# Attention and a feed-forward layer in one kernel: q and k loaded straight into the layout that the transposes read, and a planner with new deadlines

## The chip, the cores and the metric

The kernel runs on one core of a Trainium2 chip. The metric is the time of one execution on the device, in microseconds (us), the median of three runs. The profile comes from one further execution, which took 375.98 us; its span, from the first to the last instruction, is 374.2 us.

The engines of the core work side by side and meet at semaphores. TensorE (PE in the profile; PEld is its loading of weights) does matrix products into the PSUM buffers. VectorE (DVE) and ScalarE (ACT) take results out of PSUM and do elementwise work. GpSimd (POOL) issues most of the loads here, SyncE (SP) the transposing DMAs and the stores.

## The reference

The first half is an attention without softmax, for 8 batches, 12 heads, 448 positions and head size 64. The second is a feed-forward layer (768 to 2048 to 768) with an exact gelu over its 3,584 rows.

```python
scores = scale * np.matmul(q, k.transpose(0, 1, 3, 2))       # scale = 1 / sqrt(64)
attn = np.maximum(scores, 0.0) ** 2 / S                      # S = 448
attn_out = np.matmul(attn, v)
x = attn_out.transpose(0, 2, 1, 3).reshape(B * S, H * D)     # 3584 x 768
h = x @ w_in
g = 0.5 * h * (1.0 + erf(h / sqrt(2)))
out = g @ w_out
```

Inputs and output are float32; the kernel computes in bf16 with float32 sums.

## The kernel before

**Attention.** Heads are taken four at a time, so a batch has three groups (g = 0, 1, 2), and the keys of a group in seven blocks (i = 0 to 6). One step is one (batch, group, block): four score matmuls (`ps<-qT,kT`, L623) into a PSUM buffer named "w" in the planner, a relu with the scale that brings them to SBUF (`a_sq<-ps`: L635 on ScalarE, L637 on VectorE), and a square on VectorE (`a_sq<-a_sq`, L644). After seven steps come 28 matmuls with v (`pav`, L683), also into a "w" buffer, and two copies to `xT`. There are three "w" buffers.

**Feed-forward.** The first product (`psh`, L730) with its gelu (L740) fills a ring `h_sb` of two batches. The second (`pso`, L1036) works on groups of 256 output rows, by a scheme of seven products in place of eight (p1 to p7, in the order p1, p6, p2, p7, p5, p4, p3), with sums of h halves and of weight quarters formed on VectorE. Results pass through output buffers `osb` (L1070) and go out by DMA. The PSUM buffers of these are named "f"; there are two. The last two batches use the same seven-product scheme for their first product as well (`add_blocks`, `add_block`: matmuls `pb`, L870; passes `part`, L904; gelu L913). There a batch gives 28 atoms of six matmuls, 14 for each half of the hidden units; in a half each of the products p1, p6, p2, p7, p5, p4, p3 stands twice, for the two column halves of one "w" buffer. A pass takes a partial result out of a bank before the next product adds to it: v1 copies p1, v2 and v3 follow p6 and p7, and p4 goes into the bank that v3 has read.

**q, k and v.** Scores need q and k with the head dimension on partitions. Batches 0 and 1 are transposed on TensorE. Batches 2 to 7 take another way: GpSimd issues three DMAs that load and cast q, k and v of a batch (tiles `nq`, `nk`, `v_sb`). VectorE permutes q and k in SBUF (`pq<-nq`, L477, six copies in a batch; `pk<-nk`, L466, three copies) so that two heads lie side by side in 128 columns. SyncE then issues seven transposing DMAs (`kT<-pk`, L569, three; `qT<-pq`, L578, four). `pq` and `pk` have one buffer each, `qT` and `kT` two. After the transposes of a batch a small copy on GpSimd, the gate (L590), waits for their end; behind it stand the loads of the next batch but one after the batch that is being computed.

**The order.** A planner in Python (`Scheduler`) decides, while the program is built, in which order each engine gets its instructions. It has a model of durations. The first part, to about 50 us, is written out by hand (`ORDER`). From batch 2 on TensorE's order is fixed too: the score steps of a batch stand in six slots, two to a group (four steps with the v product of the group before in the middle, then three), and feed-forward work is spread evenly between them. In the last two batches `woven` mixes the `pb` atoms with `pso` products. What is left to the planner is the order on VectorE and ScalarE, and which of the two takes a relu or copy: each operation lists its engines, and a relu on VectorE, its second choice, is charged `RELU_DVE`, 0.8 us. From the second pass on, the choice among operations that can start within `NEAR` goes to the earliest deadline (`self.late`), which `deadlines` works out backwards from TensorE's sequence. The DMAs on GpSimd keep their written order; at most eight of them are under way at once. What the engines wait for on the chip is set by the data alone, not by the planner's times.

Of the kernel before, what the change touches and what calls it, by code (L numbers as in the profile page):

```python
# [51 lines left out]
TSUM_BIAS = 0.2  # L52
LEADS = {3: 8}
LAST = 256
PASSES = 2
NEAR = 0.5
QUEUE_STEP = 1.5
LOAD_MARGIN = 2.0


def cols(half):
# [41 lines left out]
class Scheduler:  # L103
# [39 lines left out]
    def pick(self, ops, only=None):  # L143
        top, near = None, []
        for n, op in enumerate(ops):
            t = self.ready(op)
            if t is None:
                continue
            for x, (eng, dur, lat) in enumerate(op.engines):
                if self.late and only not in (None, eng):  # L150
                    continue
                est = max(t, self.free[eng])
                if isinstance(lat, tuple):
                    est = max(est, self.landed[-8])
                if eng == "PE" and op.mode != self.mode:
                    est += SWITCH
                key = (est + op.bias + x * op.other, n)
                if top is None or key < top[0]:
                    top = (key, est, op, eng, dur, lat)
                near.append((est + x * op.other, est, n, op, eng, dur, lat))  # L160
        if top and self.late and only in ("ACT", "DVE"):
            edge = min(near)[0] + NEAR
            top = min(
                ((self.late[id(o)], n), est, o, eng, dur, lat)
                for at, est, n, o, eng, dur, lat in near if at <= edge
            )
        return top
# [26 lines left out]
    def run(self, fixed):  # L194


        for _ in range(PASSES):
            self.reset()
            self.place(fixed)
            self.deadlines()  # L200
        self.open = []
        n = len(ORDER.split())
        for est, op, eng in self.log[:n] + sorted(self.log[n:], key=lambda x: x[0]):
            op.fn(eng)

    def deadlines(self):


        after = {id(o): [] for o in self.open}
        for o in self.open:  # L210
            for d in o.deps:
                if id(d) in after:
                    after[id(d)].append(o)
                elif isinstance(getattr(d, "op", None), Op):
                    after[id(d.op)].append(o)
        takers = {}
        for _, o, _ in self.log:
            for name in o.need:
                takers.setdefault(name, []).append(o)
        for name, v in self.given.items():  # L220
            n = self.buffers[name]
            for x, o in enumerate(v):
                if x + n < len(takers[name]):
                    for y in [o] + list(o.joint):
                        after[id(y)].append(takers[name][x + n])
        self.late = {}
        t = math.inf
        order = sorted(self.log, key=lambda x: x[0])
        pe = [o for _, o, e in order if e == "PE"]
        ideal, at = {}, 0.0  # L230
        for o in pe:
            ideal[id(o)] = at
            at += o.engines[0][1]
        shift = pe[-1].start - ideal[id(pe[-1])]
        queue = math.inf
        for est, o, e in reversed(order):
            t = ideal[id(o)] + shift if e == "PE" else est + 50.0
            if e == "SP" and o.mode == "X":
                t = min(t, queue - QUEUE_STEP)
            for s in after[id(o)]:  # L240
                if id(s) in self.late:
                    t = min(t, self.late[id(s)] - (o.done - o.start))
            if e == "SP" and o.mode == "X":
                queue = t
            self.late[id(o)] = t
# [38 lines left out]
def kernel(  # L284
# [55 lines left out]
    def kv_view(t, b, g0, g1):  # L340

        return t[b, 4 * g0 : 4 * g1].rearrange("h s d -> (h s d)").rearrange(
            "(x p f) -> p x f", p=128, f=NK * D
        )
# [21 lines left out]
    def get_p():  # L366
        if not pqk:
            pqk.append(natpool.tile([KC, NC, DM], BF16, tag="pq", name="pq"))
            pqk.append(natpool.tile([128, G, NK * 128], BF16, tag="pk", name="pk"))
        return pqk  # L370
# [29 lines left out]
    def dma(fn, nbytes, deps=(), issues=1):  # L400
        op = sch.add((("POOL", 0.7 * issues, (nbytes, issues)),), lambda e: fn(), deps)
        pool_q.append(op)
        return op
# [7 lines left out]
    def war(b):  # L411

        old = [o for (bb, *_), o in list(Pq.items()) + list(Pk.items()) if bb == b - 1]
        c = {1: -1, 2: 0}.get(b, b - 1)
        old += [o[0] for (bb, *_), o in list(Tq.items()) + list(Tk.items()) if bb == c]
        return old

    def add_k(b, g0, g1):
        def fn():
            get_nat(b)  # L420
            nc.gpsimd.dma_start(nk[b][:, 2 * g0 : 2 * g1], kv_view(k, b, g0, g1))

        o = dma(fn, (g1 - g0) * 4 * S * 256, war(b))
        for g in range(g0, g1):
            ld_k[b, g] = [o] * NK
# [10 lines left out]
    def add_v(b, g0, g1):  # L436
# [6 lines left out]
        for g in range(g0, g1):  # L443
            ld_v[b, g] = [o]

    def add_load(b, g0=0, g1=G):
        add_k(b, g0, g1)
        add_q(b, g0, g1)
        add_v(b, g0, g1)
# [29 lines left out]
    def add_pk(b, g0, g1, after=(), bias=0.0):  # L479
        for g in range(g0, g1):  # L480
            deps = ld_k[b, g] + list(after)
            deps += [Tk[max(b - 1, 1), x, i][0] for x in range(G) for i in range(NK)]
            Pk[b, g] = sch.add(
                (("DVE", 0.31, 0.43),),
                lambda e, g=g: permute_k(V.tensor_copy, g, nk[b][:, 2 * g : 2 * g + 2]), deps,
                bias=bias,
            )

    def add_pq(b, g0, g1, c0=0, c1=NC, after=(), bias=0.0):
        for g in range(g0, g1):  # L490
            deps = [ld_q[b, g, c] for c in range(c0, c1)] + list(after)
            deps += [Tq[max(b - 1, 1), g, c][0] for c in range(c0, c1)]
            if b == 2:
                deps += [Tq[1, x, c][0] for x in range(G) for c in range(NC)]
            d = 2 * (0.07 + (c1 - c0) * 128 / 3840)

            def fn(e, g=g):
                permute_q(
                    V.tensor_copy, g, c0, c1, nq[b][:, 4 * g : 4 * g + 4, c0 * D : c1 * D]
                )  # L500

            op = sch.add((("DVE", d, d + 0.12),), fn, deps, bias=bias)
            for c in range(c0, c1):
                Pq[b, g, c] = op
# [354 lines left out]
    def add_block(b, m4, y, ms, bank, x, t, TS, xs, old, half):  # L859
# [39 lines left out]
        def passed(name, to, other, deps, need=()):  # L899
            def fn(e):  # L900
                if other is None:
                    copy(e, get(to), ps(name))
                else:
                    V.tensor_add(get(to), ps(name), get(other))  # L904

            eng = e_copy(S, 1)
            return sch.add(eng if other is None else eng[:1], fn, deps, need=need, bias=PASS_BIAS)

        def gelu(src, r, c, deps, frees=()):
            def fn(e):  # L910
# [376 lines left out]
    def at(b, n):  # L1287
        return [at_slot(b, n)]
# [5 lines left out]
    for b in range(2, B):  # L1294
        add_steps(steps(b), dve=True)
        if b == 2:
            x1 = f1(1)
            first_atoms = x1[:LEAD]
            flow += x1[LEAD:]
            flow += [(2.6, add_plain(t, n)) for n in (1, 0) for t in (0, 1)]  # L1300
            add_tsums()
        elif b in F1B:
            flow += f1(F1B[b])
        if b + 1 < B:

            n = {2: 2, 3: 2}.get(b, 1)
            add_pk(b + 1, 0, G, after=at(b, n) + SUMS[0] + SUMS[1])
            add_pq(b + 1, 0, G, after=at(b, n) + SUMS[0] + SUMS[1])
            add_T_dma(b + 1, [at(b, n + (y >= 4)) for y in range(7)])
            if b + 2 < B:  # L1310
                add_gate(b + 1)
                add_load(b + 2)
        flow += [y for g in GROUPS.get(b, ()) for y in add_group(g)]
    add_wsums(at(B - 1, 1), [F1[B - 3, m, None] for m in range(KF)])

    def woven(x, y, n):


        tx, ty, gone, out = sum(o[0] for o in x), sum(o[0] for o in y[:n]), 0.0, []
        k = 0  # L1320
        for o in x:
            out.append(o)
            gone += o[0]
            while k < n and (k + 0.5) / n < gone / tx:
                out.append(y[k])
                k += 1
        return out + y[k:]

    end = woven(add_blocks(B - 2), add_group(9), 4)
    g10 = add_group(10)  # L1330
    end += g10 + woven(add_blocks(B - 1), add_group(11), 4)
    end += add_group(12) + add_group(13)
    pe_q.extend(x[1] for x in first_atoms)
    share, gone, edge = sum(x[0] for x in flow) / (B - 2), 0.0, 0.0
# [50 lines left out]
```

## Time and profile before

| | |
|---|---|
| time, median of 3 (lowest to highest) | 376.32 us (376.17 to 376.45) |
| span of the profiled execution | 374.2 us |
| TensorE's granted clock, mean | 1.000 |
| DMA packets | 69,685, of which 30,512 on the queue of GpSimd |
| idle before the gate copies, for the transposes | 155.6 us in 5 waits |

```profile
DVE  3998981799848787985889768946888879785762
ACT  4998864746337865666546575657562333035100
PEclk9999999999999999999999999999999999999999
DMA  9999999997579969989333799400020201210233
q0 software_dynamic: 30512, 22.47, 40.2%
q1 hardware_dynamic: 38768, 19.46, 25.5%
L635 ACT ACTIVATE a_sq<-ps 128x896 bf16<-128x896 f32 (+1 forms) x143 | 122.8, 914 | 57.5 <-PE ps L623 57.5
L637 DVE TENSOR_SCALAR a_sq<-ps 128x896 bf16<-128x896 f32 x26 | 28.2, 1088 | 28.5 <-PE ps L623 28.1
L590 POOL COPY gate<-qT 128x4 bf16<-128x4 bf16 x5 | 1.3, 266 | 155.6 <-DMA qT<-pq 155.6
nk<-in_k_dram POOLq DMA_DIRECT2D x5, 672.0 KB, 6.7
nq<-in_q_dram POOLq DMA_DIRECT2D x5, 672.0 KB, 9.3
v_sb<-in_v_dram POOLq DMA_DIRECT2D x5, 672.0 KB, 13.4
```

In the first four lines the span is cut into 40 slices of some 9.4 us, and a digit is the busy share in tenths (for PEclk the granted clock). The queue lines give packets, MB and the time of the packets as a share of 16 DMA engines' span. In a line of a group of instructions there stand after the bar the busy time and the mean duration in ns, and after the second bar the idle time just before them with what ended it. In the last three, the size of one DMA and the median time from its issue to its landing.

### The profile page before, as it was taken

How to read it: one execution, taken by the hardware profiler on the slowest of the kernel's cores; microseconds unless marked ns; L12 is line 12 of the kernel's file. 1: busy time of each engine (PE TensorE's matmuls, PEld its weight loads, DVE VectorE, ACT ScalarE, POOL GpSimd, SP SyncE). 2: the span in 40 equal slices, each digit the busy share in tenths (PEclk: the TensorE clock that was granted, in tenths of full speed). 3: DMA queues.
4: the chain of work that ended last, by engine and by line, in shares of the span. 5: the costliest groups of instructions: out<-in, count | busy, mean ns of one | idle time of the engine just before them, and what ended most of it. 6: DMA issues, size and time to landing. Idle time of an engine off the chain costs nothing.

```text
span 374.2 us, 8324 instructions
## 1 busy us (share of the span) xinstructions
PE 363.0 (97%) x3485; PEld 215.4 (58%) x3485; DVE 284.3 (76%) x517; ACT 200.9 (54%) x301; POOL 46.0 (12%) x69
## 2 busy tenths in 40 slices
PE   8799999999999999999999999999999999999995
PEld 7566645455554455544555445544555886688663
DVE  3998981799848787985889768946888879785762
ACT  4998864746337865666546575657562333035100
POOL 8666400300002011002000020000000000000000
PEclk9999999999999999999999999999999999999999
DMA  9999999997579969989333799400020201210233
GB/s 175 195 201 204 202 190 114 171 205 143 94 171 162 146 75 190 238 113 159 64 101 79 140 154 181 120 3 0 2 86 12 75 2 31 90 49 2 85 86 84
DMA packets 69685, 42.96 MB, mean 115 GB/s; under 512 B 37776, under 2 KB 66192, under 8 KB 69648
## 3 DMA queue, kind: packets, MB, share of 16 engines
q0 software_dynamic: 30512, 22.47, 40.2%
q1 hardware_dynamic: 38768, 19.46, 25.5%
q8 instruction: 27, 0.44, 0.5%
q10 hardware_dynamic: 368, 0.51, 0.4%
q14 instruction: 10, 0.08, 0.1%
HBM read 45.61 MB, written 11.01 MB: 151 GB/s over the span
## 4 chain that ended last, share of the span: by engine, by line
PE 84%; DVE 6%; ACT 4%; issue 2%; DMA 2%; POOL 1%; DVEq 0%; ACTq 0%; POOLq 0%
PE pso L1036 32%; PE psh L730 29%; PE ps L623 8%; PE pb L870 7%; PE pav L683 4%; ACT a_sq L635 4%; PE pso L1131 3%; DVE a_sq L644 3%; DVE part L904 2%; DMA nk<-in_k_dram 2%; DVE a_sq L637 1%; DVE xT L387 0%; DVE kT L387 0%; PE tp L517 0%; ACT xT L389 0%
## 5 line engine op out<-in xcount | busy, mean ns | idle before, releaser
L635 ACT ACTIVATE a_sq<-ps 128x896 bf16<-128x896 f32 (+1 forms) x143 | 122.8, 914 | 57.5 <-PE ps L623 57.5
L730 PE MATMUL psh<-xT,win_sb 128*128 128x448 bf16 (+1 forms) x612 | 114.2, 342 | 0.1
L644 DVE TENSOR_TENSOR a_sq<-a_sq 128x896 bf16<-128x896 bf16 (+1 forms) x169 | 98.7, 615 | 11.2 <-ACT a_sq L635 10.1
L730 PEld LDWEIGHTS <-win_sb 128*128 128x128 bf16 x612 | 57.4, 98 | 53.7 <-issue 9.2
L740 ACT ACTIVATE h_sb<-psh 128x448 bf16<-128x448 f32 x96 | 52.5, 547 | 34.3 <-PE psh L730 34.0
L1036 PEld LDWEIGHTS <-s_sb 128*128 128x128 bf16 x424 | 40.6, 98 | 27.7 <-issue 2.5
L623 PE MATMUL ps<-qT,kT 64*64 64x448 bf16 (+1 forms) x756 | 48.5, 336 | 3.1 <-ACT a_sq L635 0.7
L637 DVE TENSOR_SCALAR a_sq<-ps 128x896 bf16<-128x896 f32 x26 | 28.2, 1088 | 28.5 <-PE ps L623 28.1
L1036 PEld LDWEIGHTS <-h_sb 128*128 128x128 bf16 x312 | 29.8, 98 | 20.9 <-issue 2.4
L1036 PE MATMUL pso<-wout_sb,h_sb 128*128 128x384 bf16 x208 | 38.1, 326 | 0.0
L1036 PE MATMUL pso<-t_sb,s_sb 128*128 128x384 bf16 x208 | 38.1, 326 | 0.0
L1036 PE MATMUL pso<-wout_sb,s_sb 128*128 128x384 bf16 (+2 forms) x216 | 38.1, 320 | 0.0
L683 PE MATMUL pav<-a_sq,v_sb 64*64 64x448 bf16 (+1 forms) x756 | 36.8, 330 | 0.8 <-ACT a_sq L635 0.4
L623 PEld LDWEIGHTS <-kT 64*64 64x64 bf16 x756 | 18.6, 105 | 26.9 <-issue 21.3
L1070 DVE TENSOR_TENSOR osb<-pso,p_sb 128x384 f32<-128x384 f32 x39 | 21.6, 555 | 9.5 <-PE pso L1036 7.3
L683 PEld LDWEIGHTS <-v_sb 64*64 64x64 bf16 x756 | 21.1, 107 | 13.1 <-issue 2.3
L387 DVE CAST xT<-pav 128x448 bf16<-128x448 f32 (+1 forms) x44 | 24.3, 582 | 5.5 <-PE pav L683 4.9
L904 DVE TENSOR_TENSOR part<-pb,part 128x448 f32<-128x448 f32 x40 | 23.1, 618 | 6.3 <-PE pb L870 6.2
L913 ACT ACTIVATE h_sb<-part 128x448 bf16<-128x448 f32 x24 | 13.3, 577 | 18.4 <-DVE part L904 18.3
L590 POOL COPY gate<-qT 128x4 bf16<-128x4 bf16 x5 | 1.3, 266 | 155.6 <-DMA qT<-pq 155.6
L870 PEld LDWEIGHTS <-win_sb 128*128 128x128 bf16 x192 | 18.4, 98 | 3.2 <-issue 2.1
L1036 PE MATMUL pso<-t_sb,h_sb 128*128 128x384 bf16 x104 | 19.0, 326 | 0.0
(60 smaller groups left out, 262.1 us busy)
## 6 DMA issues: line engine op xcount, KB each, us to landing
nk<-in_k_dram POOLq DMA_DIRECT2D x5, 672.0 KB, 6.7
nq<-in_q_dram POOLq DMA_DIRECT2D x5, 672.0 KB, 9.3
v_sb<-in_v_dram POOLq DMA_DIRECT2D x5, 672.0 KB, 13.4
out_dram<-osb SPq DMA_DIRECT2D x8, 336.0 KB, 3.1
wout_sb<-in_moe_w_out_dram POOLq DMA_DIRECT2D x2, 1152.0 KB, 11.7
v_sb<-in_v_dram POOLq DMA_DIRECT2D x9, 224.0 KB, 9.0
out_dram<-osb SPq DMA_DIRECT2D x7, 288.0 KB, 3.1
out_dram<-osb SPq DMA_DIRECT2D x8, 240.0 KB, 2.8
```

The source lines that it names most:

```text
L387: V.tensor_copy(dst, src)
L623: nc.tensor.matmul(ps[64 * j : 64 * j + 64, e, x * w : x * w + w], kT[r, g, i * 128 + 64 * j : i * 128 + 64 * j + 64], qT[r, 2 * g + j, co ...
L635: A.activation(ar, ps, AF.Relu, scale=c_att)
L637: V.tensor_scalar(ar, ps, c_att, 0.0, op0=mybir.AluOpType.mult, op1=mybir.AluOpType.max,)
L644: V.tensor_mul(box["a2"][:, :, :used], ar, ar)
L683: nc.tensor.matmul(pav[0][o2 : o2 + 64, e, :w], vt[b][r, 2 * g + e, bass.ts(i, D)], box["a2"][r, e, o : o + w], start=(i == 0), stop=(i == ...
L730: nc.tensor.matmul(ph[:, x * n : x * n + n], win_sb[:, kd, bass.ts(m + x, 128)], xT[b][:, kd, c], start=(kd == 0), stop=(kd == KD - 1),)
L740: A.activation(h_ring()[:, m : m + nm, o + c.start : o + c.stop], box[0][:, :S].rearrange("p (x n) -> p x n", x=nm), AF.Gelu,)
L870: nc.tensor.matmul(bank[name][:, y, z * HS : z * HS + HS], w[:, k, bass.ts(mm, 128)], right()[:, k], start=first and k == 0 and z == 0, st ...
L904: V.tensor_add(get(to), ps(name), get(other))
L1036: nc.tensor.matmul(box[bank][:, n0:n1], left()[:, kf], right[:, kf, n0:n1], start=bool(need) and kf == 0, stop=kf == K2 - 1, skip_group_ch ...
L1070: V.tensor_add(out()[:, n0:n1], box[bank][:, n0:n1], other()[:, n0:n1])
```

## The change

**Loads.** `add_load` of batches 3 to 7 becomes `add_wide`. It loads q and k from DRAM straight into `pq` and `pk`, 64 elements at a time: six DMAs for k (two places of a head in a pair, three groups), twelve for q, and one for v as before. The permuting copies of these batches (`add_pk`, `add_pq`) and their tiles are dropped; the transposes wait for the DMAs instead (`Both` stands for several DMAs as one). Batch 2 keeps its copies. `WIDE` is the factor by which the planner reckons such a load dearer.

**Deadlines.** `deadlines` took each TensorE operation's ideal time from the sum of the durations before it, shifted to end with the last one. It now takes the end of the operation just before it in the last pass, that is, the time at which it could start without a wait. `limit` is the latest end of each operation. A relu's charge for VectorE falls away when its first engine, ScalarE, would end more than `LIMIT` past that. There are five passes instead of two, and the one in which TensorE ends earliest is used. A transpose's deadline gets a margin of 5 us.

**The end.** `woven` puts one `pso` product behind the fourth and tenth of each 14 atoms, where it went by summed durations before. The first copies (v1) in the blocks may run on ScalarE alone, where both engines were allowed.

```diff
-PASSES = 2
+PASSES = 5
+LIMIT = 0.1
+QUEUE_MARGIN = 5.0
+WIDE = 2.0
...
-                near.append((est + x * op.other, est, n, op, eng, dur, lat))
+                other = op.other
+                if x and self.late:
+                    first = max(t, self.free[op.engines[0][0]]) + op.engines[0][2]
+                    if first > self.limit[id(op)] + LIMIT:
+                        other = 0.0
+                near.append((est + x * other, est, n, op, eng, dur, lat))
...
+            end = self.free["PE"]
+            if best is None or end < best[0]:
+                best = (end, list(self.log))
...
             ideal[id(o)] = at
-            at += o.engines[0][1]
-        shift = pe[-1].start - ideal[id(pe[-1])]
+            at = o.start + o.engines[0][1]
...
-            t = ideal[id(o)] + shift if e == "PE" else est + 50.0
+            t = ideal[id(o)] if e == "PE" else est + 50.0
...
-                    t = min(t, self.late[id(s)] - (o.done - o.start))
+                    m = QUEUE_MARGIN if e == "SP" and o.mode == "X" else 0.0
+                    t = min(t, self.late[id(s)] - (o.done - o.start) - m)
+            self.limit[id(o)] = t + (o.done - o.start)
...
+    def add_wide(b):
...
+                to = get_p()[1].rearrange("p g (i e d) -> e p g i d", e=2, d=D)
+                src = kv_view(k, b, 0, G).rearrange("p (g e) (i d) -> e p g i d", e=2, d=D)
+                for g in range(G):
+                    nc.gpsimd.dma_start(to[e][:, g], src[e][:, g])
...
+                to = get_p()[0].rearrange("p c (g j e d) -> j e g p c d", j=2, e=2, d=D)
+                src = q[b].rearrange("(g e j) (p c) d -> j e g p c d", e=2, j=2, c=NC)
+                for g in range(G):
+                    nc.gpsimd.dma_start(to[j][e][g], src[j][e][g])
...
     def add_load(b, g0=0, g1=G):
+        if b > 2:
+            return add_wide(b)
...
-            return sch.add(eng if other is None else eng[:1], fn, deps, need=need, bias=PASS_BIAS)
+            return sch.add(eng[1:] if other is None else eng[:1], fn, deps, need=need, bias=PASS_BIAS)
...
-            add_pk(b + 1, 0, G, after=at(b, n) + SUMS[0] + SUMS[1])
-            add_pq(b + 1, 0, G, after=at(b, n) + SUMS[0] + SUMS[1])
...
-            while k < n and (k + 0.5) / n < gone / tx:
-                out.append(y[k])
-                k += 1
+            if n % 14 in (3, 9):
+                out.append(y.pop(0))
```

More of the change, by code (lines that the diff above doesn't have):

```diff
@@ L194, in run @@
     def run(self, fixed):
+        best = None
         for _ in range(PASSES):
@@ L200, in run @@
             self.deadlines()
-        self.open = []
+            end = self.free["PE"]
+            if best is None or end < best[0]:
+                best = (end, list(self.log))
+        self.open, self.log = [], best[1]
         n = len(ORDER.split())
@@ L225, in deadlines @@
                         after[id(y)].append(takers[name][x + n])
-        self.late = {}
-        t = math.inf
+        self.late, self.limit = {}, {}
         order = sorted(self.log, key=lambda x: x[0])
@@ L444, in add_v, with k_fn, fn, q_fn @@
             ld_v[b, g] = [o]
+    def add_wide(b):
+        def k_fn(e):
+            def fn():
+                to = get_p()[1].rearrange("p g (i e d) -> e p g i d", e=2, d=D)
+                src = kv_view(k, b, 0, G).rearrange("p (g e) (i d) -> e p g i d", e=2, d=D)
+                for g in range(G):
+                    nc.gpsimd.dma_start(to[e][:, g], src[e][:, g])
+            return fn
+        def q_fn(e, j):
+            def fn():
+                to = get_p()[0].rearrange("p c (g j e d) -> j e g p c d", j=2, e=2, d=D)
+                src = q[b].rearrange("(g e j) (p c) d -> j e g p c d", e=2, j=2, c=NC)
+                for g in range(G):
+                    nc.gpsimd.dma_start(to[j][e][g], src[j][e][g])
+            return fn
+        def v_fn():
+            vt[b] = vpool.tile([128, HP, NK * D], BF16, tag="v", name="v_sb")
+            nc.gpsimd.dma_start(vt[b], kv_view(v, b, 0, G))
+        n = G * 4 * S * 256
+        ks = [dma(k_fn(e), WIDE * n / 2, war(b), G) for e in range(2)]
+        qs = [dma(q_fn(e, j), WIDE * n / 4, war(b), G) for e in range(2) for j in range(2)]
+        old = [o for (bb, *_), o in AV.items() if bb == b - 3]
+        o = dma(v_fn, n, old)
+        ops = Both(ks), Both(qs)
+        for g in range(G):
+            ld_v[b, g] = [o]
+            Pk[b, g] = ops[0]
+            for c in range(NC):
+                Pq[b, g, c] = ops[1]
+    class Both:
+        def __init__(self, ops):
+            self.ops = ops
+        @property
+        def done(self):
+            ends = [o.done for o in self.ops]
+            return None if None in ends else max(ends)
     def add_load(b, g0=0, g1=G):
+        if b > 2:
+            return add_wide(b)
         add_k(b, g0, g1)
@@ L1314, with woven @@
     add_wsums(at(B - 1, 1), [F1[B - 3, m, None] for m in range(KF)])
[L1316 to L1321, printed above, removed]
+    def woven(x, y):
+        out, y = [], list(y)
+        for n, o in enumerate(x):
             out.append(o)
-            gone += o[0]
-            while k < n and (k + 0.5) / n < gone / tx:
-                out.append(y[k])
-                k += 1
-        return out + y[k:]
-    end = woven(add_blocks(B - 2), add_group(9), 4)
+            if n % 14 in (3, 9):
+                out.append(y.pop(0))
+        return out + y
+    end = woven(add_blocks(B - 2), add_group(9))
     g10 = add_group(10)
-    end += g10 + woven(add_blocks(B - 1), add_group(11), 4)
+    end += g10 + woven(add_blocks(B - 1), add_group(11))
     end += add_group(12) + add_group(13)
```

## The prediction

> **What bounds the kernel now.** I read the engine totals and the row of 40 slices first, then the chain of work that ended last, then windows and the timeline around each place where that chain leaves TensorE. In the totals TensorE is busy for 97% of the span, VectorE for 76%; ScalarE's 54% falls to a third or less near the end.
>
> ```profile
> PE 363.0 (97%) x3485; PEld 215.4 (58%) x3485; DVE 284.3 (76%) x517; ACT 200.9 (54%) x301; POOL 46.0 (12%) x69
> ...
> PE 84%; DVE 6%; ACT 4%; issue 2%; DMA 2%; POOL 1%; DVEq 0%; ACTq 0%; POOLq 0%
> ```
>
> So only what shortens TensorE's gaps counts. Gaps before 31 us lie in the hand-written opening order, which the change leaves alone. From there to about 290 us the chain is an unbroken row of matmuls, but for ten detours of this shape:
>
> ```profile
> 140.79 0.60 issue
> 141.39 0.92 ACT a_sq L635
> 142.36 0.38 PE ps L623 x4
> ```
>
> The timeline around this one shows their size:
>
> ```profile
> 140.14 0.57 PE L623 MATMUL ps<-qT,kT 64*64 64x448 bf16 x8
> 140.29 0.55 DVE L1070 TENSOR_TENSOR osb<-pso,p_sb 128x384 f32<-128x384 f32 x1
> ...
> 140.58 2.62 ACT L635 ACTIVATE a_sq<-ps 128x896 bf16<-128x896 f32 x3 [0.86 <-PE ps L623]
> 140.76 0.68 DVE L1017 TENSOR_TENSOR s_sb<-s_sb,h_sb 128x1024 bf16<-128x1024 bf16 x1
> ...
> 141.87 0.87 PE L623 MATMUL ps<-qT,kT 64*64 64x448 bf16 x8
> ```
>
> The same eight score matmuls take 0.57 us at 140.14 and 0.87 us at 141.87: the second group of four waits for a "w" buffer whose relu is the second in ScalarE's queue. That is 0.30 us, ten times: **3.0 us**. (They stand near 89, 124, 132, 142, 154, 191, 204, 241, 265 and 278 us.)
>
> In the blocks of the last two batches the gaps end at VectorE:
>
> ```profile
> 331.62 1.31 PE L870 MATMUL pb<-xs,ws 128*128 128x224 bf16 x12
> 331.82 2.84 DVE L904 TENSOR_TENSOR part<-pb,part 128x448 f32<-128x448 f32 x5 [0.18 <-PE pb L870]
> ...
> 333.03 0.48 PEld L870 LDWEIGHTS <-win_sb 128*128 128x128 bf16 x5 [0.26 <-issue]
> ```
>
> p4 needs both passes (v3) over bank b; they take 1.15 us from 331.82 and the two p5 beside them are as long, so 0.26 us stays open. It comes four times (near 297, 309, 333, 344 us), and once, at 300.09 us, 0.74 us more: **1.8 us**. All that this change can win is thus 3.0 + 1.8 = 4.8 us.
>
> **What the skill says.** "DMA: Bandwidth & Descriptors", section Why small descriptors are slow: a packet costs its 32-byte beats and about 3 cycles more; its section Where 436 GB/s comes from gives 850 MHz. For this kernel's reads of 1,792 and 1,024 bytes that makes 59 and 35 cycles, 69.4 and 41.2 ns. The trace agrees: 204 and 199 GB/s written, over 16 engines, in packets of 896 and 512 bytes are 70 and 41 ns (third column from the left is PE; DMA share and GB/s stand last):
>
> ```profile
> 79.00:81.00 2.00, 2.00 (x14) 1.22 (x13) 2.00 (x4) 0.58 (x2) 0.00 (x0) 1.00 1.26 204
> 82.00:85.00 3.00, 3.00 (x28) 1.49 (x26) 2.96 (x5) 0.64 (x1) 0.00 (x0) 1.00 1.45 199
> ```
>
> The same page's Specifications warn that under 512 bytes a transfer is read, modified and written; no 128-byte packet is in the trace before. "SBUF — State Buffer", the box on VectorE blocking DMA, says that VectorE's two-port copies keep GpSimd from writing descriptors. The permuting copies, SBUF to SBUF in bf16, may be such; GpSimd's issues keep to 0.82 to 0.95 us beside a VectorE busy by 80%, so I see nothing of it here and count nothing.
>
> **The change, part by part.**
>
> 1. Permuting copies of batches 3 to 7 go.
>
> ```profile
> L477 DVE COPY pq<-nq 112x512 bf16<-112x512 bf16 x36 | 8.1, 284 | 0.4 <-DMA nq<-in_q_dram 0.4
> L466 DVE COPY pk<-nk 128x896 bf16<-128x896 bf16 x18 | 6.6, 384 | 1.5 <-DMA nk<-in_k_dram 1.5
> ```
>
> Batch 2 keeps 6 and 3, so 30 x 0.284 + 15 x 0.384 = 14.3 us of durations leave VectorE (12.2 us of busy time, as neighbours overlap). It isn't the bound: this pays only through part 3.
>
> 2. Loads. For a batch, k was one DMA of 768 packets of 896 bytes (768 x 70 / 16 = 3.4 us), q one of 1,344 of 512 (3.5 us). Now both come in runs of 64 elements: 2 x 5,376 = 10,752 packets, 256 bytes read and 128 written. Low end by the skill's formula: 11 cycles, 12.9 ns, 8.7 us. High end, if each costs double for the short write: 17.4 us. Also 18 DMAs instead of 2 must be issued: the trace has 0.73 us for 448 packets (the thirds of q) and 0.82 us for 768, so 12 x 0.73 + 6 x 0.83 = 13.7 us of GpSimd. I take 14 us, set by the issue, and some 3 us to land: q is there 17 us after the gate (before: 10.4), v after about 20 (before: 15.4).
>
> What is queued behind? On GpSimd v, then the next gate. On SP the seven transposes of the batch, behind them stores of output rows; then all score matmuls of the batch. As pq and pk are single buffers, a load can now start only after the transposes of the batch before, but the gate copy imposed that already:
>
> ```profile
> POOL gate L590 <- DMA qT<-pq: 155.6, 5, 44.0
> ```
>
> Batch 4 is tightest. Its load starts at 112.0 us after the gate of batch 3, its transposes land by 138.9, its first scores run at 140.1. With mine: q at 129, seven transposes at about 1.3 us each behind v (132), done by 137 to 141. But batch 3's transposes also come sooner: before, they waited for permuting copies at 97.6 to 103.5, though its loads had landed at 90.1. They can start near 95 and end near 105, and batch 4 gains that: done near 131 to 134. Batches 5 to 7 have 10, 0 and 13 us between transposes and scores before; there too the copies, not the data, had set the start (194 to 204 us, for loads landed at 183.0). Cost on the path: nothing, hidden behind FFN matmuls.
>
> 3. Deadlines and late relus. A relu of 1.09 us (VectorE) instead of the second 0.92 us one (ScalarE) in a queue ends the detours if VectorE is free at the right moment. At 140.6 to 142.4 us above it does a subtraction of h halves and an output pass; with 14.3 us less to do there is room for ten such relus (10.9 us), though some will collide with passes that free "f" buffers. The model can now let a relu go to VectorE when ScalarE would miss the deadline, and its deadline is where the preceding TensorE work ends. I take two thirds: **2.0 us** of the 3.0. Ends: 0 (the waits move to pso) and 3.0.
>
> 4. The end. The third-group products are put in after atoms 4 and 10 of each 14, instead of by time. Hence eight pso matmuls (1.30 us) always stand between p5 and p4: more than the 0.26 us that p4 waits. And p4's two halves now stand together, so the second needn't wait for the pass over the first, which was the 0.74 us. First copies (v1) move to ScalarE, 6 x 0.62 us off VectorE for 6 x 0.53 us; their taker p2 is 2.4 us away behind p6 and pso. **1.7 us** of the 1.8; ends: 1.0 and 1.8.
>
> 5. Five passes with the best kept, and the margin before a transpose, run in the planner and cost nothing on the chip.
>
> Sum: 376.3 - 2.0 - 1.7 - 0.0 = **372.6 us**.
>
> **Rivals.**
>
> Gains only at the end, 375 us. VectorE takes more relus, but output passes queue behind them and pso products wait in turn for "f": 376.3 - 1.7 + 0.4. For it: at the detours VectorE was mostly busy with just these passes. Against: twelve relus on it between 80 and 290 us made no such wait, and it has 14.3 us less to do.
>
> Loads too slow, 381 us (slower). If short writes cost 17.4 us and batch 3's transposes come no sooner, batch 4 lands v at 112 + 2 + 17.4 + 3.4 = 135, transposes end at 144 and scores wait 4 us. At 32 ns a packet (22 us; the durations of single packets, 88 and 60 ns at 896 and 512 bytes, extrapolated) they'd wait 8.5 us: 376.3 - 3.7 + 8.5 = 381. For it: 10,752 packets for 2,112, and a warning on the page. Against: 20 us and more in most batches.
>
> A new order that loses, 378 us. A transpose early in SP's queue blocks stores, output buffers run out, product passes wait. For it: every issue on SP is in order. Against: the loads land before the place at which the transposes ran.
>
> **How the numbers follow.** Forecast 0.64, end only 0.16, slow loads 0.10, lossy order 0.10. The first is faster; of the second I give 0.12 to faster and 0.04 to no change; of the lossy order 0.02 to no change and 0.08 to slower; slow loads are slower. Faster 0.76, same 0.06, slower 0.18. The low end is all gaps gone, 376.3 - 4.8 = 371.5, less 0.3 for spread; the high end, 378.5, takes in the second case and half of the lossy order.
>
> **What would show it.** VectorE's total falls by some 5 us at least; about 43,000 packets more on the software queue; q and v land 15 to 22 us after each gate; first scores of each batch follow FFN matmuls without a gap; fewer than four 0.30 us detours; no gap before p4. Wrong would be: a gap over 1 us before a batch's first scores (loads), or new waits of pso on osb passes (order).

## The result and the profile after

The changed kernel takes 372.04 us (371.94 to 372.19), the kernel before 376.38 us beside it: ratio 0.9886, 95% interval 0.9869 to 0.9903. That is 4.3 us less, where 3.7 us had been forecast. The profiled span fell from 374.2 to 370.0 us.

The engine totals and the shares of the chain that ended last, of the kernel after:

```profile
PE 360.5 (97%) x3485; PEld 215.0 (58%) x3485; DVE 279.4 (76%) x475; ACT 196.2 (53%) x298; POOL 108.8 (29%) x149
...
PE 92%; DMA 4%; POOL 1%; ACT 1%; issue 1%; DVE 0%; POOLq 0%; DVEq 0%; ACTq 0%
```

TensorE runs the same 3,485 matmuls. What changed is the chain: its share rose from 84% to 92%, and VectorE's 6% went to zero. VectorE has 45 permuting copies fewer (12.2 us of busy time) and six first copies fewer (3.7 us), yet only 4.9 us less to do: ten relus more, of 1.09 us each, fill the rest. GpSimd is busy for 62.8 us more, nearly all of it issues of DMAs.

The places shown before, in the timeline of the kernel after. First score steps of batch 4:

```profile
139.04 0.57 PE L685 MATMUL ps<-qT,kT 64*64 64x448 bf16 x8
139.19 0.55 DVE L1132 TENSOR_TENSOR osb<-pso,p_sb 128x384 f32<-128x384 f32 x1
...
139.47 0.92 ACT L697 ACTIVATE a_sq<-ps 128x896 bf16<-128x896 f32 x1 [0.86 <-PE ps L685]
139.66 1.09 DVE L699 TENSOR_SCALAR a_sq<-ps 128x896 bf16<-128x896 f32 x1
...
140.67 0.68 DVE L1079 TENSOR_TENSOR s_sb<-h_sb 128x1024 bf16<-128x1024 bf16 x1
140.76 0.55 PE L685 MATMUL ps<-qT,kT 64*64 64x448 bf16 x8
```

The second relu now starts on VectorE at 139.66, right behind the output pass, instead of a subtraction of h halves. It ends at 140.75, and the eight score matmuls after it take 0.55 us where they took 0.87. Of ten such detours two are left, and in the chain of the kernel after they look as before:

```profile
262.38 0.92 ACT a_sq L697
...
274.91 0.92 ACT a_sq L697
```

In the blocks at the end, p4 (the first line of `pb<-xs,win_sb` below) follows the product that now stands ahead of it:

```profile
294.70 1.46 PE L1098 MATMUL pso<-t_sb,s_sb 128*128 128x384 bf16 x8
294.90 1.16 DVE L966 TENSOR_TENSOR part<-pb,part 128x448 f32<-128x448 f32 x2
...
296.00 1.31 PE L932 MATMUL pb<-xs,win_sb 128*128 128x224 bf16 x12
```

The passes behind p5 run from 294.90 beside the product, and both halves of p4 (twelve matmuls) go through in one piece. None of the five gaps before p4 is left. In sum eight detours of 0.30 us and the gaps of 1.8 us make 4.2 us, which is the difference of the spans.

### The profile page after: what moved, and what is told of

It reads as the page before. It is cut to its first block, busy times and chain, and to the rows that moved or that the text cites. A ratio compares the mean times of both kernels' runs of the same rounds, so it can differ in the third digit from the quotient of the medians.

```text
span 370.0 us, 8385 instructions
## 1 busy us (share of the span) xinstructions
PE 360.5 (97%) x3485; PEld 215.0 (58%) x3485; DVE 279.4 (76%) x475; ACT 196.2 (53%) x298; POOL 108.8 (29%) x149
## 4 chain that ended last, share of the span: by engine, by line
PE 92%; DMA 4%; POOL 1%; ACT 1%; issue 1%; DVE 0%; POOLq 0%; DVEq 0%; ACTq 0%
PE pso L1098 32%; PE psh L792 30%; PE ps L685 9%; PE pb L932 9%; PE pav L745 8%; PE pso L1193 3%; DMA v_sb<-in_v_dram 2%; DMA nk<-in_k_dram 2%; ACT a_sq L697 1%; POOL nk L433 0%; POOL v_sb L451 0%; POOL nq L348 0%; PE tp L579 0%; ACT kT L401 0%; DVE osb L1132 0%
## 5 line engine op out<-in xcount | busy, mean ns | idle before, releaser
L697 ACT ACTIVATE a_sq<-ps 128x896 bf16<-128x896 f32 (+1 forms) x133 | 114.5, 912 | 63.9 <-PE ps L685 63.9
L706 DVE TENSOR_TENSOR a_sq<-a_sq 128x896 bf16<-128x896 bf16 (+1 forms) x169 | 97.5, 616 | 6.1 <-ACT a_sq L697 5.4
L792 PEld LDWEIGHTS <-win_sb 128*128 128x128 bf16 x612 | 57.4, 98 | 54.2 <-issue 9.8
L699 DVE TENSOR_SCALAR a_sq<-ps 128x896 bf16<-128x896 f32 x36 | 39.1, 1090 | 37.0 <-PE ps L685 36.7
L685 PE MATMUL ps<-qT,kT 64*64 64x448 bf16 (+1 forms) x756 | 46.9, 336 | 1.7 <-ACT qT L401 0.5
L475 POOL DMA_DIRECT2D pq<-in_q_dram x60 | 41.9, 706 | 10.7 <-DVE a_sq L706 5.8
L466 POOL DMA_DIRECT2D pk<-in_k_dram x30 | 28.9, 969 | 1.0 <-issue 0.5
L399 DVE CAST xT<-pav 128x448 bf16<-128x448 f32 (+1 forms) x42 | 23.2, 581 | 5.5 <-PE pav L745 4.8
```

The lines of the kernel that those rows point to most:

```text
L399: V.tensor_copy(dst, src)
L466: nc.gpsimd.dma_start(to[e][:, g], src[e][:, g])
L475: nc.gpsimd.dma_start(to[j][e][g], src[j][e][g])
L685: nc.tensor.matmul(ps[64 * j : 64 * j + 64, e, x * w : x * w + w], kT[r, g, i * 128 + 64 * j : i * 128 + 64 * j + 64], qT[r, 2 * g + j, co ...
L697: A.activation(ar, ps, AF.Relu, scale=c_att)
L699: V.tensor_scalar(ar, ps, c_att, 0.0, op0=mybir.AluOpType.mult, op1=mybir.AluOpType.max,)
```

## The experiments

All times are medians beside the kernel before on the same chip, which had 376.05 us in the first set of four, 376.38 in the second, 376.19 in the third and 376.25 in the last. "Detours" are the 0.3 us waits of score matmuls between 80 and 290 us (waits of other matmuls are not among them); "relus" are those that VectorE did in that stretch.

| kernel | us | ratio (95%) | detours | relus |
|---|---|---|---|---|
| before | 376.38 | 1 | 10 | 12 |
| changed | 372.04 | 0.9886 (0.9869 to 0.9903) | 2 | 22 |
| loads alone | 375.52 | 0.9987 (0.9980 to 0.9993) | 8 | 16 |
| planner alone | 375.15 | 0.9976 (0.9968 to 0.9984) | 7 | 15 |
| end alone | 374.09 | 0.9943 (0.9931 to 0.9956) | 10 | 12 |
| changed, without loads | 373.45 | 0.9925 (0.9912 to 0.9939) | 7 | 15 |
| changed, without waiver | 373.98 | 0.9943 (0.9930 to 0.9957) | 8 | 16 |
| changed, with spare copies | 372.50 | 0.9898 (0.9884 to 0.9911) | 2 | 20 |
| without loads, fifth pass | 372.02 | 0.9894 (0.9878 to 0.9910) | 2 | 23 |
| the same, second run | 372.26 | 0.9892 (0.9875 to 0.9908) | 2 | 23 |
| changed, old weave | 373.34 | 0.9919 (0.9906 to 0.9933) | 2 | 22 |
| changed, later sums, ten passes | 371.77 | 0.9882 (0.9865 to 0.9898) | 0 | 25 |

**One part alone.** The theory was that the relus and the end bring the time and the loads are neutral by themselves.

```diff
     # loads alone: planner, weave and first copies of the kernel before
     def add_load(b, g0=0, g1=G):
+        if b > 2:
+            return add_wide(b)
```

> The kernel before with the direct loads of batches 3 to 7 alone; planner, end weave and first copies as before. My theory (loads are hidden, VectorE is not the bound, so they pay only through the late relus): no change, 376.4 us within 0.5, with nine to eleven detours of 0.3 us at score matmuls and the five gaps before p4 still there. Rival A (the 14.3 us that leave VectorE are what ends the detours, whatever the deadlines): 373.5 to 374.5 us, at most four detours left. Rival B (loads in 128-byte packets cost time on the path, and the rest of the change pays for it): 377 us or more, with a gap before the first scores of a batch.

375.52 us, eight detours, the five gaps before p4 unchanged; no gap before any batch's first scores. The gain is 0.5 us, two detours' worth, and a little more than the theory allowed in time and in detours. Both rivals fall: freed VectorE time alone ends two of the ten detours, and the loads cost nothing on the path.

```diff
     # planner alone: copies, weave and first copies of the kernel before
+                    if first > self.limit[id(op)] + LIMIT:
+                        other = 0.0
```

> The kernel before with the new planner alone (new deadlines, relu charge waived when late, five passes and the best kept, transpose margin); loads with permuting copies, end weave and first copies as before. My theory: most of the detours go even with the copies on VectorE, for the relus need the deadline first and VectorE time second: 374.2 to 375.2 us, three to six detours left. Rival A (the freed VectorE time is what counts): 376.0 to 376.8 us, eight or more left, or new waits on output passes in their place.

375.15 us, seven detours and one new wait of 0.3 us for an output pass, near 101 us. The time is within the theory's range, the detours are more than it allowed: the planner alone took away fewer than I had thought.

```diff
     # end alone: loads and planner of the kernel before
+            if n % 14 in (3, 9):
+                out.append(y.pop(0))
...
-            return sch.add(eng if other is None else eng[:1], fn, deps, need=need, bias=PASS_BIAS)
+            return sch.add(eng[1:] if other is None else eng[:1], fn, deps, need=need, bias=PASS_BIAS)
```

> The kernel before with the new end alone (products behind atoms 4 and 10 of 14, first copies on ScalarE). My theory: the five gaps before p4 are gone and nothing else moves: 376.4 - 1.7 = 374.7 us within 0.3. Rival (VectorE's lighter load from the dropped copies or the new order shortened the passes): 375.8 us or more, gaps before p4 remain.

374.09 us, 1.96 us less than the kernel before beside it; the five gaps are gone and the ten detours are all there. The end's part of the prediction stands, 1.8 us of it seen as gaps.

**The change without its loads.**

```diff
-        if b > 2:
-            return add_wide(b)
...
+            add_pk(b + 1, 0, G, after=at(b, n) + SUMS[0] + SUMS[1])
+            add_pq(b + 1, 0, G, after=at(b, n) + SUMS[0] + SUMS[1])
```

> The changed kernel with the direct loads undone: permuting copies of all batches back on VectorE, planner and end as changed. My theory: 372.3 to 373.3 us, that is, the loads bring at most 1.2 us beside the rest, as one to four detours come back near the copies. Rival A (freed VectorE time is what counts): 374.3 to 375 us, eight or more detours. Rival B (the loads cost time on the path): under 372.0 us.

373.45 us with seven detours, again between the cases. Loads alone end two detours and the planner alone three, but both together eight. Of the five that come back here (near 132, 154, 191, 204 and 240 us; the two of the changed kernel are there as before), the last is 15 us behind the last permuting copy, at 225 us. A VectorE busy with copies can't be the direct reason for that one. The planner's passes gave the hint. Each pass learns the deadlines from the one before. With the direct loads each moves one to three more relus to VectorE, and the fifth is the best by the planner's reckoning. With copies the fifth pass, which moves eight more at once, is reckoned 0.44 us worse than the fourth, since it expects waits near the copies, and the fourth is used. The next runs tested this.

**The waiver.**

```diff
-                    if first > self.limit[id(op)] + LIMIT:
+                    if False:
```

> The changed kernel without the waived charge: a late relu pays 0.8 us for VectorE as before; loads, deadlines, five passes and end as changed. By the planner the five passes then all give the same plan after the second, with 17 relus on VectorE between 75 and 290 us. My theory (the waiver, applied once more in each pass, is what moves the relus; freed VectorE time and new deadlines alone do not): the eight detours of the loads-only run are back, 372.0 + 6 x 0.3 = 373.8 us within 0.4. Rival (the new deadlines alone do it, or the earlier transposes): within 0.4 of the changed kernel, at most three detours.

373.98 us with the eight detours of the loads alone, as the theory said. New deadlines and five passes do nothing without it: the detours and the 16 relus are those of loads alone, and the ratio, 0.9943, is near the product of loads alone and end alone, 0.9987 x 0.9943 = 0.9930.

**Spare copies.**

```diff
+            add_spare(at(b, n) + SUMS[0] + SUMS[1])
...
+    def add_spare(after):
+        for g in range(G):
+            sch.add((("DVE", 0.31, 0.43),), lambda e: V.tensor_copy(spare()[:, :896], win_sb[:, 0, :896]), after)
```

Three double copies of 112 x 512 follow in the same way, so that a batch has nine copies as before. The spare tile is never used.

> The changed kernel, direct loads kept, with copies of the same number, shapes and durations as the permuting copies put on VectorE for batches 3 to 7 where the planner finds room; they read a weight tile and write a spare one, and nothing waits for them. My theory (what hurts beside the relus is the copies' place between the loads and the transposes, and their time only where it is short): 372.0 to 372.8 us, two to four detours. Rival (VectorE's time itself, 14 us of it, is what the detours need): 373.2 us or more, six or more detours or waits on output passes.

372.50 us, two detours, 20 relus. With all the 14.3 us of copies back on VectorE the detours stay away. Time on VectorE is not what decides.

**Permuting copies with the fifth pass's plan.**

```diff
     # without loads, as above
-            if best is None or end < best[0]:
+            if True:
```

> The changed kernel with permuting copies instead of the direct loads (as in the run without loads), but the fifth pass's plan used instead of the best of five: 24 relus on VectorE instead of 16. My theory (copies and late relus get into each other's way on VectorE): fewer detours than the seven of that run, but longer waits of TensorE near 100, 131, 142 and 203 us, 373.4 to 374.5 us in all. Rival (the choice of the pass was the planner's mistake, and relus and copies do fit): 372.0 to 372.8 us.

372.02 us (0.9894, interval 0.9878 to 0.9910): the rival is right, relus and copies do fit, and the choice of the fourth pass was the planner's mistake. But the profiled execution, at 373.72 us the slowest of five, had two waits of 0.7 and 0.8 us that neither theory nor rival had. Its timeline there:

```profile
148.23 1.47 PE L1096 MATMUL pso<-t_sb,s_sb 128*128 128x384 bf16 x8
149.65 0.56 DVE L1130 TENSOR_TENSOR osb<-pso,p_sb 128x384 f32<-128x384 f32 x1 [2.22 <-DMA out_dram<-osb]
...
150.26 1.46 PE L1096 MATMUL pso<-t_sb,h_sb 128*128 128x384 bf16 x8 [0.56 <-DVE osb L1130]
```

An output pass waits 2.22 us for the store that frees its buffer, and the next product waits for the pass. The store, issued at 142.6 us, landed at 149.6 beside the loads of batch 5. To know whether this is the rule, the same kernel ran again beside the changed one:

> The changed kernel itself, on the same chip as the next run, as its measure: 372.0 us within 0.4, two detours near 263 and 275 us.

> The permuting copies with the fifth pass's plan again, beside the changed kernel. Theory after the first seven runs (the direct loads gain nothing on the chip by themselves; they gain because the planner, with copies to place, picks a plan with fewer late relus): within 0.4 us of the changed kernel; of detours and waits for output passes at most 1.2 us between 80 and 290 us. Rival (the 1.5 us of waits for output buffers in the profile of the earlier run, behind stores that share the DMA engines with a load, are the rule, so direct loads do gain): 1 us or more above the changed kernel, with these waits near 150 us again.

372.13 us (0.9893, interval 0.9878 to 0.9908) and 372.26 us (0.9892, interval 0.9875 to 0.9908). The wait near 150 us is there again, but only of 0.5 us; with one of 0.3 us near 101 us and the two detours the waits make 1.4 us, a little over what I had allowed. In their times the two kernels can't be told apart.

In their spans they can: 369.9 to 370.2 us for the changed kernel, 370.2 to 370.7 for the other. The two waits for output passes, 0.8 us together, are in the second alone. The one near 101 us is in all four runs that join permuting copies and new planner (both runs with the fifth pass, the planner alone, the change without loads), and in each the pass stands right behind permuting copies on VectorE. Against that, what of the time lies outside the span is 2.2 us in the changed kernel and 1.7 in the other; no run shows why. So the direct loads by themselves gain about half a microsecond of span and nothing that shows in the time; the rest is what the planner makes of them.

The groups of relus on VectorE between 80 and 290 us, in the changed kernel, in the change without loads, and with the fifth pass:

```profile
L699 DVE TENSOR_SCALAR a_sq<-ps 128x896 bf16<-128x896 f32 x22 | 24.0, 1090 | 28.1 <-PE ps L685 28.1
```

```profile
L697 DVE TENSOR_SCALAR a_sq<-ps 128x896 bf16<-128x896 f32 x15 | 16.4, 1091 | 24.0 <-PE ps L683 24.0
```

```profile
L697 DVE TENSOR_SCALAR a_sq<-ps 128x896 bf16<-128x896 f32 x23 | 25.0, 1089 | 21.5 <-PE ps L683 21.5
```

22 and 23 relus with two detours each, 15 with seven: few detours go with many relus on VectorE, whether q and k are permuted by copies or by the loads.

**The end.**

```diff
-            if n % 14 in (3, 9):
-                out.append(y.pop(0))
+            while k < n and (k + 0.5) / n < gone / tx:
+                out.append(y[k])
+                k += 1
```

> The changed kernel with the old weave at the end, first copies still on ScalarE. My theory (the product placed between p5 and p4 covers the passes): the gaps before p4 are back, four of 0.26 us and perhaps the one of 0.7: 373.2 to 373.9 us. Rival (the first copies on ScalarE freed VectorE and shortened the passes): within 0.4 us of the changed kernel.

373.34 us; the four gaps of 0.26 us are back, the one of 0.74 is not. So the new weave is what closes the four. The fifth stays away here with the old weave, while it was there in the runs with the loads alone and with the planner alone. What it was can be read from the kernel before:

```profile
298.56 0.95 DVE L794 TENSOR_TENSOR ws<-ws,win_sb 128x1536 bf16<-128x1536 bf16 x1
299.42 0.61 DVE L904 TENSOR_TENSOR part<-pb,part 128x448 f32<-128x448 f32 x1
300.09 0.54 PE L870 MATMUL pb<-xs,win_sb 128*128 128x224 bf16 x4 [0.52 <-DVE part L904]
```

A weight sum of 0.95 us got onto VectorE ahead of the last pass, and the second half of p4 waited for that pass. With the old weave and the first copies on ScalarE the same sum runs ahead of all the passes:

```profile
292.81 0.96 DVE L856 TENSOR_TENSOR ws<-ws,win_sb 128x1536 bf16<-128x1536 bf16 x1
294.28 2.84 DVE L966 TENSOR_TENSOR part<-pb,part 128x448 f32<-128x448 f32 x5 [0.52 <-PE pb L932]
```

That the first copies, gone from VectorE, made the room for it is likely; they were not moved by themselves, so this stays open.

**Loads in half the run length.**

```diff
-                    nc.gpsimd.dma_start(to[e][:, g], src[e][:, g])
+                    for h in (slice(0, 32), slice(32, 64)):
+                        nc.gpsimd.dma_start(to[e][:, g, :, h], src[e][:, g, :, h])
```

The same for q; the planner counts the double number of issues.

> The changed kernel with q and k of batches 3 to 7 loaded in runs of 32 elements: 36 DMAs and 21,504 packets of 64 bytes a batch instead of 18 and 10,752 of 128. My theory (the loads are hidden with some 10 us to spare at batch 4, and their length is that of the issues): issues take 28 us instead of 14; the first scores of batch 4 wait 4 to 10 us, later batches little: 375 to 383 us. Rival (loads have far more room than that, as the planner's queues float): within 1 us of the changed kernel. Third case (packets under 128 bytes cost no less than those of 128, and the DMA engines set the pace): over 384 us, with waits at several batches.

397.88 us (1.0568, interval 1.0529 to 1.0607), worse than my range and in that of the third case. TensorE's waits in this run:

```profile
PE ps L687 <- DMA qT<-pq: 20.1, 4, 14.1
```

And the timeline at batch 4:

```profile
139.65 2.58 SPq L1061 DMA_DIRECT2D out_dram<-osb  x4
143.78 7.03 SPq L642 DMA_TRANSPOSE qT<-pq  x4
153.07 0.96 PE L687 MATMUL ps<-qT,kT 64*64 64x448 bf16 x8 [14.07 <-DMA qT<-pq]
```

The third case's reason is not seen, though: GpSimd's issues did set the pace (from 112.2 to 140.4 us, 28 us). What I had left out is what follows. v is issued last and landed at 150.5, and the four transposes of q, issued from 143.8 on, all landed behind it, by 152.8. From one gate to the next it now takes 41.3 us, more than the 37 us of a batch, so the next batches wait again. The rest of the loss is the clock's (last section). The direct loads are hidden, but their room is about 10 us at this batch: in the changed kernel transposes end at 128.9 and scores start at 139.0.

**A further step.** Of the two detours left, the one at 262 us stands beside a weight sum of the last batches (0.95 us on VectorE, from 261.38). The other, at 274 us, stands between subtractions of h halves and output passes.

```diff
-    add_wsums(at(B - 1, 1), [F1[B - 3, m, None] for m in range(KF)])
+    add_wsums(at(B - 1, 2), [F1[B - 3, m, None] for m in range(KF)])
...
-PASSES = 5
+PASSES = 10
```

> The changed kernel with the weight sums of the last batches placed one slot later and ten passes instead of five. The two detours left (263 and 275 us) stand beside these sums on VectorE. My theory (a detour stays where VectorE cannot start a relu at once): the one at 263 us goes and 275 stays, 371.7 us within 0.25. Rival (what is left has another cause, or the sums then hold up the first blocks near 287 us): 372.0 us or more.

371.77 us, ratio 0.9882 (0.9865 to 0.9898), and both detours are gone, where the theory had expected one to stay. It is 0.3 us under the changed kernel, with overlapping intervals; two detours are worth 0.6. The run makes two edits at once, so which of them ended which detour is not shown.

## Why the prediction was right

**What bounds the kernel.** Right. TensorE's gaps were all there was to win: 4.8 us forecast as the most, 4.2 won, and all of it at the ten detours and five gaps.

**Copies dropped.** The amount was right, 45 copies of 14.3 us. Part 3 then leaned on it ("with 14.3 us less to do there is room for ten such relus"), and that step is wrong as a reason. Ten more relus did come, but that the number fits is luck. Spare copies of the same size left two detours, and permuting copies with another plan did too. What the copies took in the main was not VectorE's time but the planner's consent: with them it reckoned the plan with late relus as worse.

**Loads.** Hidden, as forecast. The terms: I had 0.73 and 0.83 us per issue, they took 0.70 for q and 0.97 for k, so 14.2 us instead of 13.7. q of batch 4 landed 18.7 us after its gate (17 forecast), v 22.7 (20). In the other batches v took 22 to 35 us, more than the 22 that the prediction allowed; it cost nothing, as no batch had to wait for its scores. The gate of batch 3 came at 103.1 us, where I had its transposes end near 105, and the transposes of batch 4 ended at 128.9 (131 to 134). The price of a packet was nearer the low end. Between 109 and 113 us 149 GB/s were written, which over 16 engines is 13.7 ns for 128 bytes. The Trainium skill's page "DMA: Bandwidth & Descriptors", section Why small descriptors are slow, has 11 cycles for such a packet, an estimate of 12.9 ns at the 850 MHz of its section Where 436 GB/s comes from. The doubling feared for short writes did not show:

```profile
109.00:113.00 4.00, 4.00 (x28) 1.85 (x26) 0.00 (x0) 1.63 (x3) 4.00 (x7) 1.00 2.35 149
```

The last number but one says that an engine had 2.35 packets under way at a time. A single packet thus took some 2.35 x 13.7 = 32 ns, just what the slow-load rival extrapolated. Its mistake was to count them one after the other.

**Deadlines and late relus.** The mechanism was right, the size small by 0.4 us: eight of ten detours, 2.4 us, not two thirds. Without the waived charge the planner's part does nothing beside the loads; the waiver with the old deadlines was not run. The passes matter because each turns up further late relus.

**The end.** 1.7 us forecast, 1.8 in gaps, 1.96 measured alone. My reason for the 0.74 us gap, that p4's two halves stand together, is not borne out: with the old weave they stand apart, and the gap is gone all the same. I had overlooked the weight sum ahead of the pass.

**Rivals.** No product waits for "f" behind relus in the changed kernel, no batch waits for its scores, no store holds up a pass. Late loads can cost more than the slow-load rival feared, but it took twice the issues, and the issues set the pace, not the price of a packet.

## What to carry to other kernels

Where an engine at 97% is the bound, list its gaps by size and by releaser: their sum caps what a change that leaves its own work alone can bring, and it told within 0.6 us what this one did. A greedy planner that chooses among its own plans can lose more by the choice than by the work: before a piece of work is taken off an engine to make room, run the plan that the model rejects. A load in many small DMAs from GpSimd was here about as long as its issues, so count them first, and count what stands behind them in the same loop.

## What the runs showed of the hardware

TensorE's granted clock falls in a long wait, or just after a shorter one, and takes time to return; a wait of under 3 us is enough. In the run with half-length loads, around the wait of 14.07 us that ended at 153.07, and around the later one of 2.70 us (PEclk is the third column from the right, TensorE's busy time stands behind the stretch's length; the fifth line, from the timeline, is the wait itself):

```profile
144.00:153.00 9.00, 0.00 (x0) 0.00 (x0) 0.00 (x0) 0.00 (x0) 0.00 (x0) 0.50 1.12 188
153.10:157.40 4.30, 4.30 (x45) 2.15 (x46) 1.80 (x3) 1.25 (x2) 4.02 (x6) 0.50 0.79 30
157.50:170.00 12.50, 12.50 (x115) 6.95 (x114) 10.83 (x20) 5.25 (x7) 12.50 (x16) 1.00 1.50 87
...
229.20:231.80 2.60, 0.00 (x0) 0.00 (x0) 0.00 (x0) 0.54 (x1) 0.00 (x0) 1.00 0.70 148
231.85 0.57 PE L687 MATMUL ps<-qT,kT 64*64 64x448 bf16 x8 [2.70 <-DMA qT<-pq]
232.60:235.90 3.30, 3.30 (x37) 1.68 (x27) 1.81 (x3) 1.46 (x2) 3.30 (x4) 0.50 0.91 34
236.00:240.00 4.00, 4.00 (x23) 2.05 (x21) 2.15 (x5) 2.58 (x5) 4.00 (x6) 1.00 1.54 58
```

After the long wait TensorE works at half clock for 4.4 us more. After the wait of 2.70 us, through which the clock shows 1.00, it is at half for some 3.4 us, and after one of 2.78 us near 273 us the same again. The Trainium skill's page "TensorE: Matmul & The Clock Gate", section Part 1: The HAM clock gate, has the clock at half rate when TensorE has been idle for a window of some 3.4 us, and full again after a busy one. The length of the half-rate stretches agrees. The 2.70 and 2.78 us waits are shorter than that window and halved the clock all the same, so here the measurement decides.

A wait of some 3 us so costs about 1.7 us more than itself, one of 14 us about 2.2. That run lost 25.8 us against the changed kernel: 20.1 are waits for transposes, and 11.2 us at half clock are worth 5.6 us, together 25.7. In the kernel before and in the changed one the clock shows 1.00 up to the last slices.
